# Matmuls of a zeroed tile ahead of and between the first score chunks of an attention and gated feed-forward kernel

## The chip, the cores and the metric

The kernel runs on one core of a Trainium2 chip. The metric is the device time of one launch in microseconds (us). The engines are named as in the profile: PE (TensorE, matmul), PEld (TensorE's loading of weights, which overlaps PE), DVE (VectorE), ACT (ScalarE), POOL (GpSimd) and SP (SyncE, which here issues most of the early DMAs).

## The reference

```python
def _attn_ref(q, k, v) -> np.ndarray:          # (4, 8, 1152, 64) each
    B, H, S, D = q.shape
    factor = 2
    scale = 1.0 / np.sqrt(D)
    q_pool = q.reshape(B, H, S // factor, factor, D).mean(axis=3)
    scores = scale * np.matmul(q_pool, k.transpose(0, 1, 3, 2))
    scores = scores - np.max(scores, axis=-1, keepdims=True)
    attn = np.exp(scores)
    attn = attn / (np.sum(attn, axis=-1, keepdims=True) + 1e-09)
    return np.matmul(attn, v).astype(np.float32)

def _moe_ref(x, w_in, w_out) -> np.ndarray:    # x (2304, 512), d_ff 2048
    h = x @ w_in
    sp = np.where(h > 20.0, h, np.log1p(np.exp(np.minimum(h, 20.0))))
    g = h * np.tanh(sp)
    return (g @ w_out).astype(np.float32)
```

The pooled query gives 576 rows of scores per head against 1152 keys; the attention output of all heads, laid side by side, goes through a feed-forward block.

## The kernel before

The attention is cut into 32 steps: a batch, a pair of heads, and one half of the pooled rows (288 columns a head). Step `i` has nine score chunks of 128 keys each. A chunk (`QK(i, c)`, line 164) is two float32 matmuls, one per head, on the upper and lower half of the array's rows; the trace shows them as four records, two for each head. They write one PSUM tile `s`. ACT copies each chunk to SBUF (`CP`, line 174, into `TA` for chunks 0 to 5 and `TB` for 6 to 8). DVE keeps a running maximum (`MX`, line 185; the last fold `MXF`, line 189). After the ninth chunk PE transposes that maximum (`MT`, line 200, tile `mt`), DVE reduces it (`TMAX`, line 206, tile `m`), PE spreads the result over the partitions (`MB`, line 217, tile `Mb`), DVE subtracts it (`SUB`, line 223), ACT takes the exponential (`EXP`, line 227), and PE multiplies by the values (`PV`, line 246, tile `pv`). Steps overlap: the first chunks of step 1 stand among the last of step 0. A chunk is named (step, chunk) below.

The score tiles have two PSUM buffers (tag `S`); in step 0 chunks 1, 4 and 7 use the buffer that `mt` and `Mb` use later. So a chunk waits until ACT has copied, and DVE has read, the chunk that held its buffer before. The tags `x` and `pv` of the pool `ps1` have one buffer each.

The order on each engine is not found by a scheduler: `mode.enter_context(tc.manual_schedule())` takes the instructions as the program issues them. The program sorts a table of (time, function, arguments), whose first part is `FILL`, and calls the functions in that order. `first()` runs ahead of it:

```python
x = ps1.tile([P, 4, P], F32R, tag="x", name="warm")
for n in range(NWARM):
    pe.transpose(x[:, n % 4], identr, identr)
```

`identr` is an identity that POOL makes and DVE casts. Between the copies of the first chunks ACT, DVE and POOL also convert the first pieces of the feed-forward weights (`conv`, lines 347 to 396, tile `ri` and `wt`), which come by DMA. The steps of the attention take the first half of the time, the feed-forward (float32r matmuls, lines 433 to 727) the rest, with some overlap.

Of the kernel before, what the change touches and what calls it, by code (L numbers as in the profile page):

```python
# [8 lines left out]
F32 = mybir.dt.float32  # L9
F32R = mybir.dt.float32r  # L10
# [13 lines left out]
def tile_pooled_attention_then_winograd_ffn(ctx: ExitStack, tc: tile.TileContext, q, k, v, moe_w_in, moe_w_out, out, outT):  # L24
# [5 lines left out]
    P = 128  # L30
# [8 lines left out]
    NU = NT // UT  # L39
    GR = ((0, 2), (2, 4), (4, 6), (6, 9))  # L40
    CA = GR[3][0]
    NWARM = 19
    TW = 768
    TH = TW // 2
    KT = TW // P
# [4 lines left out]
    pe, dve, act, pool, sp = nc.tensor, nc.vector, nc.scalar, nc.gpsimd, nc.sync  # L50

    const = ctx.enter_context(tc.tile_pool(name="const", bufs=1))
    identr = const.tile([P, P], F32R, name="identr")
    cst = const.tile([P, 2], F32, name="cst")
    one, eps = (cst[:, n:n + 1] for n in range(2))
    xT = const.tile([P, NP, NT], F32, name="xT")

# [5 lines left out]
    def open_pool(name, bufs, side="left", space=bass.MemoryType.SB):  # L63
        shut[name] = ExitStack()
        pools[name] = shut[name].enter_context(
            tc.tile_pool(name=name, bufs=bufs, side=side, space=space, reuse_waits="tile")
        )
        return pools[name]

    mode = ExitStack()  # L70
    mode.enter_context(tc.manual_schedule())
    if True:
        act.preload_act_table_set("natural_log_exp_and_others")
        make_identity(nc, xT[:, 0, 0:P])
        dve.tensor_copy(identr, xT[:, 0, 0:P])
# [25 lines left out]
        ps1 = open_pool("ps1", 1, side="right", space=PSUM)  # L101
# [29 lines left out]
        def qk_tiles(p):  # L131
            qT = pqk.tile([P, 2, HQ], F32, tag="qT", name=f"qT{p}")
            kT = pqk.tile([P, NC, P], F32, tag="kT", name=f"kT{p}")
            qk[p] = (kT, qT)
# [5 lines left out]
        def QH(n):  # L140
            (pool if n in QHP else dve).tensor_tensor(qk[0][1][:, n], raw[0][:, n, 0], raw[0][:, n, 1], ALU.add)

        def first():
            qk_tiles(0)
            if NWARM:
                x = ps1.tile([P, 4, P], F32R, tag="x", name="warm")
                for n in range(NWARM):
                    pe.transpose(x[:, n % 4], identr, identr)

        rmaxs, Mbs, pvs, pvn, accs = {}, {}, {}, {}, {}  # L150
        CHAIN, SEED, FOLD = ((1, 3, 5, 7), (4, 6, 8)), (0, 2), 8
# [6 lines left out]
        def QK(i, c):  # L158
            p, hf = divmod(i, 2)
            kT, qT = qk[p]  # L160
            spare = i == 0 and c in SPARE
            s = (ps1 if spare else psS).tile([P, 2, 512], F32, tag="Mb" if spare else "S", name=f"s{i}_{c}")
            for j in range(2):
                pe.matmul(  # L164
                    s[:, j, 0:HQ],
                    kT[64 * j:64 * j + 64, c],
                    qT[64 * j:64 * j + 64, hf],
                    start=True,
                    stop=True,
                )  # L170
            ss[i, c] = s[:, :, 0:HQ]

        def CP(i, c):
            act.copy(T(i, c), ss[i, c])  # L174
# [568 lines left out]
        for n, u in enumerate(units):  # L743
            if u[0] == 0:
                banks[u] = ("b", "a", "c") if n % 2 else ("a", "b", "c")
            else:
                x, y, z = banks[units[n - 1]]
# [35 lines left out]
        def reuse_lead():  # L783
# [9 lines left out]
            (-0.3930, QH, 0),  # L793
            (-0.3740, load_w, 0),
            (-0.3510, QK, 0, 0),
            (-0.2560, QK, 0, 1),
            (-0.2360, CP, 0, 0),
            (-0.2160, load_q, 0, 1),
            (-0.1770, QK, 0, 2),
            (-0.1570, CP, 0, 1),  # L800
            (-0.1270, load_w, 1),
# [1765 lines left out]
        for u in units:  # L2567
            if 2 <= u[1] <= NFP - 2:
                for t, fn, *a in STEADY[u[0] > 0]:
                    a = (4 * u[1] + a[0], a[1]) if fn is conv else (u, *a)  # L2570
                    if (fn, *a) not in alone:
                        plan.append((NS + (at + t) / PER, fn, *a))
            at += SPANS[u[0] > 0]
        first()
        plan.sort(key=lambda e: e[0])
        for _, fn, *a in plan:
# [40 lines left out]
```

## Time and profile before

| | us |
|---|---|
| median of 3 runs | 785.08 |
| lowest and highest of them | 784.74, 788.81 |
| the profiled execution's own time | 784.51 |
| its span, first to last instruction | 782.7 |
| PE busy in the span | 767.4 (98%) |
| DVE, ACT, POOL busy | 680.6, 642.1, 654.3 |

The span is 1.8 us shorter than the profiled execution's time. A share of busy time is an average over the whole; the change touches only the first 20 us or so, where PE is less busy than later: the first of the 40 slices of the page (19.6 us each) shows seven tenths for PE, all later ones nine but the last. The profile also gives the clock that TensorE was granted, as a share of 2.4 GHz: 1.00 is 2.4 GHz and 0.50 is 1.2 GHz. The ends of matmuls are modelled, so a matmul's duration is longer than the step from one to the next.

### The profile page before, as it was taken

The numbers are of one execution on the slowest core, as the hardware profiler recorded it, in microseconds if no ns is written. First come the engines' busy times: TensorE is split into PE (matmuls) and PEld (weight loads), VectorE is DVE, ScalarE is ACT, GpSimd is POOL, SyncE is SP. The second block draws the span as 40 slices with busy tenths as digits, with TensorE's granted clock in tenths as the row PEclk, the third lists the DMA queues.
The fourth block names the chain that finished last, engine by engine and source line by source line (L and its number), as shares of the span: only waits on it lengthen the run. The fifth ranks groups of instructions, "written<-read, shape, count | busy, mean of one in ns | idle before, by whom it ended". The sixth has DMA issues, their size and how long they took to land.

```text
span 782.7 us, 14324 instructions
## 1 busy us (share of the span) xinstructions
PE 767.4 (98%) x5123; PEld 558.1 (71%) x5123; DVE 680.6 (87%) x959; ACT 642.1 (82%) x1110; POOL 654.3 (84%) x505
## 2 busy tenths in 40 slices
PE   7999999999999999999999999999999999999998
PEld 5454555545555454555557988899899999999998
DVE  5999999999999999999976778877778889587876
ACT  6999999999999999999885887777677687877762
POOL 4679988989889898988887598886788899998884
PEclk9899999999999999999999999999999999999999
DMA  7556575565755656455432788874664232254242
GB/s 269 166 152 142 176 176 116 143 151 138 181 111 149 152 137 170 116 148 116 111 69 46 241 277 290 284 257 172 192 210 151 95 121 69 95 172 142 95 132 101
DMA packets 44470, 121.90 MB, mean 156 GB/s; under 512 B 4592, under 2 KB 16368, under 8 KB 44400
## 3 DMA queue, kind: packets, MB, share of 16 engines
q1 hardware_dynamic: 34608, 71.45, 27.5%
q0 software_dynamic: 4608, 28.31, 18.4%
q10 hardware_dynamic: 5184, 21.24, 8.0%
q8 instruction: 40, 0.66, 0.3%
q14 instruction: 30, 0.25, 0.1%
HBM read 70.65 MB, written 22.02 MB: 118 GB/s over the span
## 4 chain that ended last, share of the span: by engine, by line
PE 86%; DVE 3%; ACT 3%; DMA 3%; POOL 2%; issue 1%; SPq 0%; ACTq 0%; DVEq 0%; POOLq 0%
PE s L164 20%; PE pv L246 17%; PE ma L616 11%; PE O L727 8%; PE OAy L678 7%; PE mc L616 6%; PE O L678 6%; PE mb L616 3%; PE Sb L268 2%; DMA acc<-TB 2%; PE mt L200 2%; PE h L433 1%; PE Mb L217 1%; PE OZ L710 1%; POOL acc L238 1%
## 5 line engine op out<-in xcount | busy, mean ns | idle before, releaser
L164 PE MATMUL s<-qT,kT 64*128 64x288 f32 x1152 | 205.4, 454 | 4.0 <-ACT TB L174 1.8
L164 PEld LDWEIGHTS s<-qT,kT 64*128 64x128 f32 x1152 | 94.0, 189 | 99.8 <-DVE rmax L185 24.9
L174 ACT COPY TA<-s 128x576 f32<-128x576 f32 x192 | 117.9, 638 | 22.9 <-PE s L164 16.5
L223 DVE TENSOR_TENSOR TA<-TA,Mb 128x1152 f32<-128x1152 f32 x96 | 128.9, 1347 | 1.9 <-PE Mb L217 1.0
L227 ACT ACTIVATE TA<-TA 128x1152 f32<-128x1152 f32 x96 | 112.8, 1176 | 4.1 <-DVE TA L223 3.6
L246 PE MATMUL pv<-TA,vn 128*64 128x288 f32 x768 | 115.2, 422 | 0.8 <-ACT TA L227 0.8
L232 POOL TENSOR_TENSOR acc<-TA 128x1152 f32<-128x1152 f32 x32 | 85.0, 2656 | 36.2 <-PE s L164 19.1
L185 DVE TENSOR_TENSOR rmax<-s,rmax 128x576 f32<-128x576 f32 x128 | 93.3, 749 | 2.1 <-ACT TB L174 1.8
L238 POOL TENSOR_TENSOR acc<-acc 128x576 f32<-128x576 f32 x64 | 91.9, 1436 | 3.9 <-DMA acc<-TB 2.6
L246 PEld LDWEIGHTS pv<-TA,vn 128*64 128x64 f32 x768 | 47.2, 137 | 48.5 <-issue 9.7
L691 DVE TENSOR_TENSOR xT<-xT,OAy 128x384 f32<-128x384 f32 x104 | 54.7, 548 | 11.9 <-PE OAy L678 11.6
L223 DVE TENSOR_TENSOR TB<-TB,Mb 128x1728 f32<-128x1728 f32 x32 | 62.2, 1944 | 0.0
L246 PE MATMUL pv<-TB,vn 128*64 128x288 f32 x384 | 61.3, 415 | 0.0
L174 ACT COPY TB<-s 128x576 f32<-128x576 f32 x96 | 59.8, 654 | 1.8 <-PE s L164 1.7
L598 POOL TENSOR_TENSOR wbl<-wS,wbh 128x1024 fp32r<-128x1024 f32 x20 | 49.5, 2476 | 5.8 <-ACT wbh L594 5.8
L227 ACT ACTIVATE TB<-TB 128x1728 f32<-128x1728 f32 x32 | 52.7, 1648 | 0.0
L185 DVE TENSOR_TENSOR rmax<-s,TA 128x576 f32<-128x576 f32 x64 | 48.3, 755 | 3.8 <-ACT TA L174 3.7
L234 POOL TENSOR_TENSOR acc<-TA 128x576 f32<-128x576 f32 x32 | 45.6, 1424 | 2.5 <-ACT TA L227 2.3
L246 PEld LDWEIGHTS pv<-TB,vn 128*64 128x64 f32 x384 | 24.0, 136 | 25.2 <-issue 11.9
L598 POOL TENSOR_TENSOR wal<-wS,wah 128x768 fp32r<-128x768 f32 x19 | 36.8, 1936 | 3.3 <-ACT wah L594 3.1
L598 POOL TENSOR_TENSOR woal<-wO,woah 128x1024 fp32r<-128x1024 f32 x13 | 31.4, 2415 | 7.9 <-ACT woah L594 6.4
L620 ACT COPY s<-ma 128x384 f32<-128x384 f32 x44 | 21.2, 482 | 20.2 <-PE ma L616 20.2
(305 smaller groups left out, 2241.3 us busy)
## 6 DMA issues: line engine op xcount, KB each, us to landing
acc<-TB POOLq DMA_DIRECT2D x32, 864.0 KB, 6.4
ri<-in_moe_w_in_dram SPq DMA_DIRECT2D x16, 512.0 KB, 4.6
ro<-in_moe_w_out_dram SPq DMA_DIRECT2D x16, 512.0 KB, 4.2
qn<-in_q_dram ACTq DMA_DIRECT2D x12, 576.0 KB, 5.0
kT<-in_k_dram ACTq DMA_DIRECT2D x12, 576.0 KB, 3.8
vn<-in_v_dram ACTq DMA_DIRECT2D x12, 576.0 KB, 4.1
wS<-sumsh SPq DMA_DIRECT2D x12, 512.0 KB, 4.0
wO<-sumso SPq DMA_DIRECT2D x13, 384.0 KB, 4.4
```

The costliest lines, as they stand in the source:

```text
L164: pe.matmul(s[:, j, 0:HQ], kT[64 * j:64 * j + 64, c], qT[64 * j:64 * j + 64, hf], start=True, stop=True,)
L174: act.copy(T(i, c), ss[i, c])
L185: dve.tensor_tensor(ss[i, c] if c == FOLD else r, ss[i, c], x, ALU.max)
L223: dve.tensor_tensor(x, x, Mbs[i].unsqueeze(1).to_broadcast([P, w, W]), ALU.subtract)
L227: act.activation(x, x, AF.Exp, scale=0.0625)
L232: pool.tensor_tensor(accs[i][:, 0:2], T(i, 0, 2), T(i, 2, 4), ALU.add)
L238: pool.tensor_tensor(accs[i][:, 0], accs[i][:, 0], accs[i][:, n - 2], ALU.add)
L246: pe.matmul(pvs[i][64 * j:64 * j + 64, 0:HQ], vn[:, j, c, :], T(i, c)[:, j], start=(pvn[i] == 1), stop=(pvn[i] == NC),)
L598: (dve if e == "dve" else pool).tensor_tensor(l, w_part(u, q), f32(h), ALU.subtract)
L616: pe.matmul(o, a, b, start=(new and m == 0), stop=(last and m == len(seq) - 1), skip_group_check=True)
L678: pe.matmul(o, x, y, start=(n == 0 and i not in CHAIN_O[1:]), stop=(n == 2 and i not in CHAIN_O[:3]), skip_group_check=True)
L727: pe.matmul(o, x, y[:, f], start=(f == 0 and m == 0), stop=(f == 1 and m == 2))
```

## The change

A tile `zeros` of 128 by 128 float32r is set to zero by DVE as its first instruction. The 19 transposes of the identity ahead of the first chunk become 29 matmuls of `zeros` by `zeros`. They write a tile on the tag `pv` in place of `x`. The same matmuls are then issued in groups behind seven of the first chunks: 4 behind (0,4), 6 behind (0,5), 6 behind (0,6), 8 behind (0,7), 8 behind (1,0), 10 behind (0,8) and 12 behind (1,1), 54 in all. Nothing reads what they write.

```diff
-    NWARM = 19
+    NWARM = 29
+    FILLER = {(0, 4): 4, (0, 5): 6, (0, 6): 6, (0, 7): 8, (1, 0): 8, (0, 8): 10, (1, 1): 12}
...
+    zeros = const.tile([P, P], F32R, name="zeros")
...
+        dve.memset(zeros.bitcast(F32), 0.0)
         act.preload_act_table_set("natural_log_exp_and_others")
...
+        turns = []
+
         def first():
             qk_tiles(0)
-            if NWARM:
-                x = ps1.tile([P, 4, P], F32R, tag="x", name="warm")
-                for n in range(NWARM):
-                    pe.transpose(x[:, n % 4], identr, identr)
+            warm(NWARM)
+
+        def warm(k):
+            if not turns:
+                turns.append(ps1.tile([P, 4, P], F32, tag="pv", name="warm"))
+            for n in range(k):
+                pe.matmul(turns[0][:, n % 4], zeros, zeros, start=True, stop=True)
...
             ss[i, c] = s[:, :, 0:HQ]
+            warm(FILLER.get((i, c), 0))
```

PE's order at the start of the program, before. `s0_4` is the score tile of chunk (0,4); `warm` is the tile that the first matmuls write.

```order
L164 MATMUL s0_0_196<-qT0_166,kT0_167 128x288 x2
L164 MATMUL s0_1_199<-qT0_166,kT0_167 128x288 x2
L164 MATMUL s0_2_204<-qT0_166,kT0_167 128x288 x2
L164 MATMUL s0_3_212<-qT0_166,kT0_167 128x288 x2
L164 MATMUL s0_4_218<-qT0_166,kT0_167 128x288 x2
L164 MATMUL s0_5_226<-qT0_166,kT0_167 128x288 x2
```

The same place on PE after the change, with the row ahead of it.

```order
L156 MATMUL warm_170<-zeros_60 128x128 x29
L172 MATMUL s0_0_208<-qT0_168,kT0_169 128x288 x2
L172 MATMUL s0_1_211<-qT0_168,kT0_169 128x288 x2
L172 MATMUL s0_2_216<-qT0_168,kT0_169 128x288 x2
L172 MATMUL s0_3_224<-qT0_168,kT0_169 128x288 x2
L172 MATMUL s0_4_230<-qT0_168,kT0_169 128x288 x2
L156 MATMUL warm_170<-zeros_60 128x128 x4
L172 MATMUL s0_5_242<-qT0_168,kT0_169 128x288 x2
```

The first five chunks stand as they did, behind 29 matmuls in place of 19 transposes; the first group follows the fifth chunk.

PE's order from chunk (0,6) to the transposes of step 0's maximum (`mt0`), before.

```order
L164 MATMUL s0_6_235<-qT0_166,kT0_167 128x288 x2
L164 MATMUL s0_7_244<-qT0_166,kT0_167 128x288 x2
L164 MATMUL s1_0_251<-qT0_166,kT0_167 128x288 x2
L164 MATMUL s0_8_255<-qT0_166,kT0_167 128x288 x2
L164 MATMUL s1_1_263<-qT0_166,kT0_167 128x288 x2
L200 MATMUL mt0_277<-identr_58,rmax0_0_210 128x64 x10
```

The same place on PE after the change.

```order
L172 MATMUL s0_6_257<-qT0_168,kT0_169 128x288 x2
L156 MATMUL warm_170<-zeros_60 128x128 x6
L172 MATMUL s0_7_272<-qT0_168,kT0_169 128x288 x2
L156 MATMUL warm_170<-zeros_60 128x128 x8
L172 MATMUL s1_0_287<-qT0_168,kT0_169 128x288 x2
L156 MATMUL warm_170<-zeros_60 128x128 x8
L172 MATMUL s0_8_299<-qT0_168,kT0_169 128x288 x2
L156 MATMUL warm_170<-zeros_60 128x128 x10
L172 MATMUL s1_1_317<-qT0_168,kT0_169 128x288 x2
L156 MATMUL warm_170<-zeros_60 128x128 x12
L209 MATMUL mt0_343<-identr_58,rmax0_0_222 128x64 x10
```

No chunk has changed its place among the others; each of these five now has a group behind it, and nothing but the score chunks' own waits stands between. ACT, POOL and SP issue the same instructions in the same order as before; DVE has one more, the memset, as its first.

## Rows read from the trace of the kernel before

**Rows 1.** The page: span, busy time, slices, and the chain of waits.

```profile
span 782.7 us, 14324 instructions
...
PE   7999999999999999999999999999999999999998
...
PEclk9899999999999999999999999999999999999999
...
PE 86%; DVE 3%; ACT 3%; DMA 3%; POOL 2%; issue 1%; SPq 0%; ACTq 0%; DVEq 0%; POOLq 0%
```

**Rows 2.** Chain of waits in order of time: start us, us, what.

```profile
2.59 5.47 DMA ri<-in_moe_w_in_dram
...
50.31 2.09 PE pv L246 x16
...
57.05 1.61 PE pv L246 x12
```

**Rows 3.** Timeline of PE: start us, us, work, idle before and its releaser.

```profile
1.62 2.65 PE L148 MATMUL warm<-identr 128*128 128x128 f32 x19 [1.62 <-DVE cst L78]
...
4.20 2.29 PE L164 MATMUL s<-qT,kT 64*128 64x288 f32 x8
...
9.40 0.76 PE L164 MATMUL s<-qT,kT 64*128 64x288 f32 x4 [0.62 <-ACT TA L174]
...
15.57 0.76 PE L200 MATMUL mt<-identr,rmax 64*128 64x64 f32 x10 [1.38 <-DVE rmax L189]
16.17 1.19 PE L164 MATMUL s<-qT,kT 64*128 64x288 f32 x8
...
21.36 1.23 PE L246 MATMUL pv<-TA,vn 128*64 128x288 f32 x4 [0.83 <-ACT TA L227]
22.52 2.15 PE L164 MATMUL s<-qT,kT 64*128 64x288 f32 x8
```

**Rows 4.** Windows: stretch, its length, PE busy (instructions), granted clock, DMA share, GB/s.

```profile
7.40:10.70 3.30, 2.58 (x18) 1.00 0.88 357
10.80:14.10 3.30, 2.72 (x16) 1.00 0.59 187
14.20:17.50 3.30, 1.78 (x18) 1.00 0.97 342
17.60:21.00 3.40, 2.83 (x17) 0.50 0.94 305
21.00:24.30 3.30, 2.94 (x12) 0.50 0.19 75
24.50:28.00 3.50, 3.50 (x26) 1.00 0.06 8
393.00:396.40 3.40, 1.55 (x14) 1.00 0.17 33
```

**Rows 5.** Timeline of ACT from 8 us.

```profile
8.09 0.78 ACT L347 ACTIVATE wt<-ri 128x512 uint16<-128x512 uint16 x1 [0.91 <-DMA ri<-in_moe_w_in_dram]
...
13.26 0.67 ACT L174 COPY TB<-s 128x576 f32<-128x576 f32 x1
14.24 0.64 ACT L174 COPY TA<-s 128x576 f32<-128x576 f32 x1 [0.31 <-PE s L164]
...
19.61 0.64 ACT L174 COPY TA<-s 128x576 f32<-128x576 f32 x1 [0.62 <-PE s L164]
```

**Rows 6.** Timeline of DVE.

```profile
13.96 0.77 DVE L185 TENSOR_TENSOR s<-s,rmax 128x576 f32<-128x576 f32 x1 [0.33 <-ACT TB L174]
...
18.54 2.62 DVE L223 TENSOR_TENSOR TA<-TA,Mb 128x1152 f32<-128x1152 f32 x2 [0.23 <-PE Mb L217]
...
24.57 1.58 DVE L185 TENSOR_TENSOR rmax<-s,rmax 128x576 f32<-128x576 f32 x2 [0.68 <-ACT TB L174]
```

**Rows 7.** Chain of waits in the feed-forward: float32r matmuls of 256 and 512 columns.

```profile
427.56 5.75 PE h L433 x48
...
499.94 2.80 PE O L727 x12
```

## The prediction

> **What bounds the kernel now.** I read the page first. PE carries 86% of the chain of waits and is nine tenths busy in every slice but the first and the last [rows 1]. From some 50 us on PE is never short of work: four more records on the chain always cost it 0.48 us (2.09 for 16 less 1.61 for 12) [rows 2]. So time won or lost in the first 30 us shifts all that follows, and nothing else in the change reaches beyond it. The reader should look for what PE, ACT and DVE wait for in those 30 us, and at PE's clock there.
>
> The granted clock is the second thing. It is 1.00 from 7.4 to 17.5 us, 0.50 (1.2 GHz) from 17.6 to 24.3, then 1.00 again [rows 4]. The profile also gives 1.00 for the first 7 us, but there durations say otherwise: eight score records from 4.20 took 2.29 us, as long as the 2.15 us at 22.52 under 0.50, while eight records at 16.17 took 1.19 [rows 3]. So the first chunks ran at 1.2 GHz too. Before the clock fell at 17.5, PE was busy 1.78 of 3.3 us with 18 instructions, ten of them small transposes, after a wait of 1.38 us for DVE; before the other fall, at 396.4, it was busy 1.55 of 3.4 us. In the two stretches from 7.4 and 10.8, with 2.58 and 2.72 us, the clock stayed [rows 3, 4].
>
> The third thing is what holds the first 16 us. The chain goes through the DMA of the first weight piece, which lands at 8.06 us [rows 2]. ACT stands on it until 8.09 with the copies of chunks (0,2) and (0,3) queued behind [rows 5]. After that ACT copies chunk after chunk; the copy of (0,8) starts at 13.26, DVE folds that chunk at 13.96, then the last maximum, and PE's transposes start at 15.57 [rows 3, 5, 6].
>
> **The change part by part.** My sums are made against the profiled execution (784.51 us: the span of 782.7 and 1.8 around it), which is 0.6 us under the median of 785.08.
>
> *29 matmuls for 19 transposes.* The transposes start at 1.62, behind POOL's identity and DVE's casts and memsets, and 19 of them take 2.65 us, at most 0.14 each [rows 3]. The new ones need only DVE's first memset, so I let them start at about 1.0. At half clock 128 columns take 0.107 us, and I bound a matmul by that and the transposes' 0.14: 29 of them end between 4.1 and 5.1 us, and the first chunk started at 4.20. That is a delay of 0 to 0.9 us for the first chunks, or a gain if the clock rises earlier. Either is hidden: ACT must wait for the weight piece until 8.09, and (0,2) and (0,3) are done by then. I take 0. The memset itself stands in front of a cast that waits for POOL's identity anyway, and the new PSUM tag has no other user before the first `pv` matmul at 21.36: 0.
>
> *What one matmul in a group costs.* No float32r matmul of 128 columns stands in the trace. At full clock 48 of 256 columns take 5.75 us, 0.120 each; 12 of 512 take 2.80, 0.233 each [rows 7]. Continued to 128 columns that is 0.120 - 0.057 = 0.063 us. The lower bound is 128 columns at 2.4 GHz, 0.053; the upper is the float32 rate: a score or `pv` matmul of 288 columns takes 0.48 us [rows 2], so 128 columns take 0.213. I take 0.064, since the float32r rows are the same kind of operand. The Trainium skill (TensorE: Matmul & The Clock Gate, Back-to-back issue gap) gives about 81 ns for N=128 in a stream of weight loads and matmuls; no run here shows it yet. By it the next sum would be 0.5 us larger.
>
> *The groups' delay.* A chunk from rest takes 0.76 us to its modelled end [rows 3] and each further one 0.48. Chunk (0,5) cannot start before 9.40, when ACT's copy frees its buffer. From there PE has (0,5), (0,6), (0,7), (1,0) and (0,8), now with 6, 6, 8 and 8 fillers between: 9.40 + 0.76 + 4 x 0.48 + 28 x 0.064 = 13.87. The copy of (0,8) would start at about 13.9 in place of 13.26 [rows 5]: 0.65 late. With 10 more fillers (1,1) ends near 15.0, and its copy, which stood at 14.24 [rows 5], is 0.8 late; ACT's two weight conversions queue behind it, then DVE's conversion, then the reduction of the maximum. The 12 last fillers end near 15.6, before the delayed maximum (16.2), so they cost nothing. The group behind (0,4) lies in PE's wait before 9.40. The delay is 0.8 us; at 0.053 a filler it is 0.5, at 0.213 see the last rival.
>
> *The clock.* If PE stayed at 2.4 GHz from 17.6 to 24.3: `Mb` and the chunk behind it come about 0.3 us sooner, taking DVE's wait of 0.23 before the subtraction and ACT's 0.62 at 19.61 with them [rows 5, 6]. The first `pv` (1.23) and the two chunks at 22.52 (2.15) halve: 1.5 us less on PE [rows 3]. DVE holds part of that back: it is busy from 18.54 on but for 0.68 us before 24.57 [rows 6], so the chain gains about 0.3 + 0.7 + 0.1 = 1.1 us, at most the 1.8 that PE alone would save.
>
> Does it stay? In the stretch that ended at 17.5, the transposes had little beside them; now the 22 last fillers and (1,1) lie there, so I expect 1.00 to hold on past 17.6. But the groups end with (1,1). The next stretch holds `Mb`, two chunks and a wait for the exponential: 2.83 us of work at half clock [rows 4], half of that at full clock, and so less than the 1.78 us that went before the fall at 17.5. I expect the clock to fall there, near 21 us, and the `pv` matmul and the two chunks at 22.52, the dear ones, to run at 1.2 GHz again. Then only some 0.3 of the 1.1 us is won, and work from 24.5 to 28 that ran at 1.00 before may run at half clock for a while, up to 0.8 us lost.
>
> Sum: +0.8 for the groups, -0.3 for the clock, 0 to +0.8 behind: +0.5 to +1.3 on 784.51, so 785.0 to 785.8. I say 785.3.
>
> **The rivals.** *The clock stays up until PE is full.* For it: 3.50 of 3.50 us busy from 24.5 on [rows 4], and the delay of 0.8 us by the groups moves real work into later stretches. Against it: the thin stretch above. Time: 784.51 + 0.8 - 1.1 = 784.2, and 783.9 at the lower price of a filler.
>
> *The zeros do not hold the clock*, because what they stream counts for nothing; no row shows matmuls of zeros. Then it falls at 17.5 again, or sooner: if the first chunks come earlier, (0,4) leaves the stretch from 7.4 and thins it. Time: 784.51 + 0.8 = 785.3 if it falls where it did, and about 787 with the chunks around 11 to 14 us at half clock as well (four of them at 0.48 more each).
>
> *Slower: a float32r matmul of so few columns runs at the float32 rate*, 0.213 us. It would be the groups that decide, between 9.40 and the transposes at 15.57. (0,8) would end at 9.40 + 0.76 + 1.92 + 5.96 = 18.0, and (1,1) with 22 more fillers at 18.0 - 0.2 + 0.48 + 4.7 = 23.0: the transposes 7.4 us late. The 29 ahead would take 6.2 to 12.4 us from 1.0 and add up to 3 us, and 1.1 would come back from the clock: 791 to 795, say 793. Slower than before by over 0.5% it is from about 0.15 us a filler. Against it stands that the transposes, also 128 columns of float32r, took at most 0.14 each at half clock [rows 3], where one pass is 0.107 and four are 0.43.
>
> **How the numbers follow.** Forecast 0.52, the clock staying up 0.24, zeros that do not hold it 0.11, the float32 rate 0.09; 0.04 for something that I have not seen. Half a per cent, about what a measurement of this kernel can tell from no change, is 3.9 us: 781.2 to 789.0. The first three cases lie inside, so "same" holds 0.87; slower is the float32 rate and the end of the third case, 0.10; faster 0.03. The range goes from 783.3, the clock staying up with PE's own saving in place of DVE's (784.51 + 0.8 - 1.8, less a little), to 788.2, the third case with a filler of 0.08. The likeliest case's own range is 784.5 to 786.3.
>
> **What would show it.** In the changed profile a group of eight fillers should take 0.5 us at full clock; the copy of (0,8) should start near 13.9 and the transposes near 16.3; PEclk should be 1.00 over 17.6 to 20.9 and 0.50 in a stretch after it. If the copy of (0,8) stays at 13.3 the groups are free and I have their price wrong; if no 0.50 stands before 30 us the first rival is right; if a group of eight takes 1.7 us the last one is. The first five chunks should be earlier or later without the 8.09 of ACT moving.

## The result and the profile after

The changed kernel took 792.44 us (median of 6 runs, 790.73 to 797.38) against 784.91 for the kernel before (median of 6, 782.70 to 788.81): a ratio of 1.0121, 95% interval 1.0095 to 1.0147. It is slower by about 1%: two of the six runs lay at 797 and lift the ratio, the two medians alone give 1.0096. The prediction had said 785.3 and "same". Run again beside the experiments (e11 below) it took 791.09, a ratio of 1.0095, 1.0081 to 1.0109. The profiled execution took 791.35 us; its span of 789.4 is 6.7 us longer than the 782.7 of before.

The page of the kernel after, the rows that answer to [rows 1] (slices, and the chain by engine and by line):

```profile
span 789.4 us, 14453 instructions
...
PE   9899999999999999999989999999999999999998
...
PEclk9999999999999999999999999999999999999999
...
PE 87%; POOL 4%; ACT 3%; DVE 3%; DMA 2%; issue 1%; ACTq 0%; DVEq 0%; POOLq 0%
PE s L172 20%; PE pv L255 16%; PE ma L625 11%; PE O L736 7%; PE OAy L687 7%; PE mc L625 6%; PE O L687 6%; PE mb L625 3%; PE Sb L277 2%; POOL acc L247 2%; PE warm L156 2%; PE mt L209 2%; PE h L442 1%; DMA acc<-TB 1%; PE OZ L719 1%
```

The first slice is full now (9 where a 7 stood), and matmuls of zeros hold 2% of the chain. PE's timeline shows where they stand (start us, us, work; in brackets idle time before it and what ended it; no row before 25 us but the first gives any). It answers to [rows 3].

```profile
1.06 6.45 PE L156 MATMUL warm<-zeros 128*128 128x128 f32 x29 [1.06 <-DVE zeros L75]
7.43 4.58 PE L172 MATMUL s<-qT,kT 64*128 64x288 f32 x20
11.94 0.66 PE L156 MATMUL warm<-zeros 128*128 128x128 f32 x4
12.54 0.76 PE L172 MATMUL s<-qT,kT 64*128 64x288 f32 x4
13.22 0.89 PE L156 MATMUL warm<-zeros 128*128 128x128 f32 x6
...
17.95 1.11 PE L156 MATMUL warm<-zeros 128*128 128x128 f32 x8
18.99 0.76 PE L172 MATMUL s<-qT,kT 64*128 64x288 f32 x4
19.67 1.33 PE L156 MATMUL warm<-zeros 128*128 128x128 f32 x10
20.93 0.76 PE L172 MATMUL s<-qT,kT 64*128 64x288 f32 x4
21.62 1.56 PE L156 MATMUL warm<-zeros 128*128 128x128 f32 x12
23.11 0.76 PE L209 MATMUL mt<-identr,rmax 64*128 64x64 f32 x10
...
35.66 0.76 PE L209 MATMUL mt<-identr,rmax 64*128 64x64 f32 x10 [0.62 <-DVE rmax L198]
```

The first chunk starts at 7.43 in place of 4.20, chunk (0,5) at 12.54 in place of 9.40, and the transposes of step 0's maximum at 23.11 in place of 15.57. Those of step 1 come at 35.66; before they stood at 29.72:

```profile
29.72 0.76 PE L200 MATMUL mt<-identr,rmax 64*128 64x64 f32 x10 [0.74 <-DVE rmax L189]
```

The chain of waits runs through the zeros (start us, us, what):

```profile
12.61 0.69 PE s L172 x4
13.29 0.82 PE warm L156 x6
...
16.29 1.04 PE warm L156 x8
17.33 0.69 PE s L172 x4
...
19.74 1.26 PE warm L156 x10
```

Two more matmuls of zeros cost 0.22 us each time, so one costs 0.11; a group of n holds 0.15 + 0.11 n of the chain, and each chunk 0.69 where chunks that follow one another take 0.48. ACT has become the engine that waits, which answers to [rows 5]: the weight piece, chunk (0,8), chunk (1,1).

```profile
10.31 0.79 ACT L356 ACTIVATE wt<-ri 128x512 uint16<-128x512 uint16 x1
...
19.79 0.64 ACT L183 COPY TB<-s 128x576 f32<-128x576 f32 x1 [1.08 <-PE s L172]
21.73 0.64 ACT L183 COPY TA<-s 128x576 f32<-128x576 f32 x1 [1.31 <-PE s L172]
```

The windows, answering to [rows 4]: stretch, length, PE, PEld, DVE, ACT and POOL busy, granted clock, DMA share, GB/s.

```profile
13.70:17.10 3.40, 3.40 (x26) 2.49 (x25) 1.84 (x4) 2.08 (x4) 1.41 (x1) 1.00 1.01 401
17.10:20.50 3.40, 3.40 (x26) 2.49 (x25) 0.71 (x2) 1.28 (x2) 0.00 (x0) 1.00 0.28 104
...
24.00:27.40 3.40, 2.69 (x25) 1.27 (x21) 3.40 (x5) 2.56 (x5) 1.63 (x2) 1.00 0.80 283
27.40:31.00 3.60, 2.60 (x18) 1.18 (x20) 3.60 (x5) 3.58 (x5) 2.75 (x2) 1.00 0.10 42
...
403.00:406.40 3.40, 3.40 (x14) 1.88 (x16) 2.92 (x3) 3.02 (x6) 3.32 (x3) 0.50 0.00 0
```

PE is busy without a gap until the transposes at 23.1, and the clock stays at 1.00 where before it stood at 0.50; it falls only at 403 us. In exchange DVE and ACT, which carry the real work, have little to do: 0.71 and 1.28 us of the 3.4 from 17.1.

### The profile page after: what moved, and what is told of

It is laid out like the page before. It is cut to its first block, busy times and chain, and to the rows that moved or that the text cites. A ratio compares the mean times of both kernels' runs of the same rounds, so it can differ in the third digit from the quotient of the medians.

```text
span 789.4 us, 14453 instructions
## 1 busy us (share of the span) xinstructions
PE 776.1 (98%) x5187; PEld 566.8 (72%) x5187; DVE 682.1 (86%) x960; ACT 642.7 (81%) x1110; POOL 654.2 (83%) x505
## 4 chain that ended last, share of the span: by engine, by line
PE 87%; POOL 4%; ACT 3%; DVE 3%; DMA 2%; issue 1%; ACTq 0%; DVEq 0%; POOLq 0%
PE s L172 20%; PE pv L255 16%; PE ma L625 11%; PE O L736 7%; PE OAy L687 7%; PE mc L625 6%; PE O L687 6%; PE mb L625 3%; PE Sb L277 2%; POOL acc L247 2%; PE warm L156 2%; PE mt L209 2%; PE h L442 1%; DMA acc<-TB 1%; PE OZ L719 1%
```

## The experiments

My first theory was that a matmul of zeros costs what loading its 128 weight columns costs, that the groups are the larger part of the slowdown, and that most of the lead (the 29 matmuls ahead) is hidden. The rivals: that the streamed columns set the price, and that the late start is carried on whole. The table gives for each kernel how much later than before the transposes of the maximum start in step 0, 1, 12 and 28, and the span's end, in its profiled execution; and in the columns POOL and PE how long, between 100 and 395 us, POOL waited for its accumulating DMA (`acc<-TB`) and PE's `Sb` matmuls then waited for POOL.

| kernel | step 0 | step 1 | step 12 | step 28 | end | POOL | PE |
|---|---|---|---|---|---|---|---|
| before | 0 | 0 | 0 | 0 | 0 | 2.2 | 0.6 |
| after | 7.54 | 5.95 | 6.14 | 6.21 | 6.70 | 3.6 | 1.6 |
| e1, lead alone | 3.02 | 2.52 | 2.51 | 4.19 | 2.80 | 6.7 | 2.6 |
| e2, groups alone | 5.34 | 3.76 | 5.00 | 4.46 | 5.41 | 0.6 | - |
| e3, 64 weight columns | 2.52 | 1.47 | 1.74 | 1.92 | 1.61 | 3.6 | 1.6 |
| e4, 64 streamed columns | 7.65 | 6.10 | 6.42 | 6.50 | 6.68 | 3.5 | 1.6 |
| e5, all transposes | 3.56 | 4.58 | 4.58 | 4.04 | 3.80 | 0.6 | - |
| e6, bfloat16 | 2.35 | 2.26 | 7.28 | 7.41 | 7.45 | 3.7 | 1.7 |
| e7, two groups in waits | 0.11 | -1.42 | -0.92 | 0.76 | 1.40 | 8.2 | 3.2 |
| e8, one group | 0.45 | -1.09 | -1.08 | 0.04 | 0.15 | 5.1 | 1.5 |
| e9, 15 ahead | 1.93 | 1.31 | 1.30 | 0.74 | 0.70 | 0.6 | - |
| e10, nothing ahead | 0.58 | 0.21 | 0.21 | -0.31 | -1.25 | 0.6 | - |
| e11, after again | 7.54 | 5.95 | 6.01 | 6.25 | 5.93 | 3.7 | 1.8 |
| e12, e6 and a buffer | 2.33 | 2.32 | 2.34 | 2.46 | 3.39 | 3.5 | 1.6 |

The column of the end carries more than the change. In six of these profiles (before, after, e2, e4, e6, e7) the clock fell once more, for 3.4 us, between 396 and 409 us. The other eight, where it did not, all gained 1.4 us on the kernel before between the transposes of steps 30 and 31. The changed kernel is on both sides (after and e11), so the code does not fix this. The column of step 28 stands ahead of it.

**e1: the lead alone.**

```diff
-    FILLER = {(0, 4): 4, (0, 5): 6, (0, 6): 6, (0, 7): 8, (1, 0): 8, (0, 8): 10, (1, 1): 12}
+    FILLER = {}
```

> Only the 29 zero matmuls ahead, no groups. In the changed kernel they took 6.45 us from 1.06 and the first chunk started at 7.43 in place of 4.20. Theory (the groups are the larger part of the loss, and most of the lead's delay is hidden by ACT's wait for the weight piece until 8.09): chunk (0,5) starts at 10.6 to 11.6 in place of 9.40, the transposes of the maximum at 16.7 to 17.8 in place of 15.57, and the time is 784.5 to 786. Rival (the late start is carried on whole): the transposes 3 us late, 787 to 788.

787.41 us against 784.09, ratio 1.0043 (1.0024 to 1.0061), and the transposes 3.02 late: my theory fell, the rival held. The 29 end as in the changed kernel and the first chunk starts at 7.43. ACT in e1:

```profile
8.81 0.64 ACT L183 COPY TA<-s 128x576 f32<-128x576 f32 x1 [6.79 <-PE s L172]
9.77 0.64 ACT L183 COPY TA<-s 128x576 f32<-128x576 f32 x1 [0.32 <-PE s L172]
10.31 0.79 ACT L356 ACTIVATE wt<-ri 128x512 uint16<-128x512 uint16 x1
```

The conversion of the weight piece, which I had used as the cover, came 2.22 us late (10.31 for 8.09) without waiting for its DMA any more, because two copies of late chunks stand ahead of it in ACT's queue. The cover was never the time until 8.09, only the 0.91 us that ACT was idle there [rows 5]: 3.2 us of lateness less 0.9 is about what is left of it there. But the conversion does not set the 3.02 us. The chain of waits in e1 passes it by: it runs from the zeros through the first four chunks to a fold of DVE, and from there to ACT's copies.

```profile
7.50 4.07 PE s L172 x16
...
11.60 0.77 DVE rmax L194
...
12.39 0.64 ACT TA L183
```

The late chunks are slow as well, for in this run the clock rose only at 11.3 us (in the changed kernel at 10.5, before at 7.3).

**e2: the groups alone.** The 19 transposes stand ahead again, the 54 zeros stay.

```diff
-            warm(NWARM)
+            x = ps1.tile([P, 4, P], F32R, tag="x", name="lead")
+            for n in range(19):
+                pe.transpose(x[:, n % 4], identr, identr)
```

> The 19 identity transposes ahead as before, and the 54 zero matmuls in groups. Theory: a group of n costs PE 0.34 + 0.112 n us at full clock, so (0,8) starts near 15.9 in place of 12.35 and the transposes of the maximum near 20.0 to 20.9 in place of 15.57; some 1.3 us come back if the clock stays at 1.00 to 30 us, which leaves 787.5 to 789. Rival (the late start is the larger part): the groups cost under 2 us, 784.5 to 786.5.

787.78, ratio 1.0041 (1.0023 to 1.0059), and the transposes at 20.91, as the theory said. The clock stayed at 1.00 from 6.0 us to 402. The two halves add up within their intervals: 1.0043 x 1.0041 is 1.0084, some 6.6 us, against 1.0095 (1.0081 to 1.0109) for the whole in e11. The first theory's order was wrong: lead and groups cost the same. One thing in e2's profile is not the groups' price: its shift grows by 1.2 us between steps 1 and 2 (3.76 to 4.99), where POOL stands 1.9 us. Run e6 shows what that is.

**e3 and e4: which half of the pair sets the price.** e3 loads 64 weight columns and streams 128; e4 loads 128 and streams 64.

```diff
-                pe.matmul(turns[0][:, n % 4], zeros, zeros, start=True, stop=True)
+                pe.matmul(turns[0][0:64, n % 4], zeros[:, 0:64], zeros, start=True, stop=True)    # e3
+                pe.matmul(turns[0][:, n % 4, 0:64], zeros, zeros[:, 0:64], start=True, stop=True) # e4
```

> As the changed kernel, but each zero matmul loads 64 weight columns in place of 128; it still streams 128. Theory (loading the weights sets the step, 256 clocks for 128 float32r columns): the step halves, to about 0.107 us at half clock and 0.056 to 0.067 at full clock; the 29 end near 4.2 and the time is 785 to 787. Rival (a float32r matmul of 128 streamed columns takes two passes or the time of 256 columns): the step stays 0.213 and 0.112, and the time 790 to 793.

> As the changed kernel, but each zero matmul streams 64 columns in place of 128; it still loads 128 weight columns. Theory (loading the weights sets the step): the step stays 0.213 us at half clock and 0.112 at full clock, and the time 790 to 793. Rival (two passes over the streamed columns): the step falls to about 0.107 and 0.056, and the time to 785 to 787. If it stays here and in the run with 64 weight columns as well, a least time for any such matmul is left.

e3 took 786.96, ratio 1.0062 (1.0030 to 1.0094); two of its eight runs lay at 794, the other six at 785.8 to 788.8, much as two of six did in the changed kernel; neither kernel has a profile of such a run. e4 took 791.65, ratio 1.0087 (1.0062 to 1.0112), in three runs. PE's timeline, the lead and the groups of 4 and 12; first e3, then e4:

```profile
1.06 3.35 PE L156 MATMUL warm<-zeros 128*64 128x128 f32 x29 [1.06 <-DVE zeros L75]
...
8.47 0.46 PE L156 MATMUL warm<-zeros 128*64 128x128 f32 x4
...
17.12 0.93 PE L156 MATMUL warm<-zeros 128*64 128x128 f32 x12
```

```profile
1.06 6.39 PE L156 MATMUL warm<-zeros 128*128 128x64 f32 x29 [1.06 <-DVE zeros L75]
...
12.27 0.63 PE L156 MATMUL warm<-zeros 128*128 128x64 f32 x4
...
21.77 1.52 PE L156 MATMUL warm<-zeros 128*128 128x64 f32 x12
```

Eight more matmuls in a group cost 0.90 us in the changed kernel (1.56 less 0.66), 0.47 with half the weight columns, 0.89 with half the streamed ones. So for this pair the load sets the price, at both levels of the clock: the lead halves with the weight columns and does not move with the streamed ones.

**e5 and e6: the same groups of another kind.** In e5 all of them, ahead and between, are transposes of the identity (19 ahead); in e6 `zeros` is bfloat16.

```diff
-                pe.matmul(turns[0][:, n % 4], zeros, zeros, start=True, stop=True)
+                pe.transpose(turns[0][:, n % 4], identr, identr)                  # e5
-    zeros = const.tile([P, P], F32R, name="zeros")
+    zeros = const.tile([P, P], mybir.dt.bfloat16, name="zeros")               # e6
```

> The same places and counts as the changed kernel, but every zero matmul is a transpose of the identity (19 ahead as before, 54 in the groups). If what costs is loading the weights of a plain float32r matmul, the transposes, which stepped by 0.127 us at half clock where the zero matmuls step by 0.213, step by 0.06 to 0.08 at full clock, the transposes of the maximum start at 17.9 to 18.9 in place of 20.9 with zero matmuls, and the time is 785 to 787. Rival (any instruction pair in a group costs 0.11, whatever it loads): 20.9, and 787 to 789.

> The changed kernel with a bfloat16 zero tile in place of float32r: 29 ahead and 54 in groups. If the load of the weights takes its time by the float32r kind (256 clocks for 128 columns), bfloat16 halves it or better: the step is 0.107 to 0.13 at half clock and 0.055 to 0.07 at full clock, the first chunk starts at 4.2 to 4.6, and the time is 785 to 787.5, as with 64 weight columns. Rival (128 weight columns take 256 clocks in any type): 0.213 and 0.112, 790 to 793.

e5: 787.43, ratio 1.0049 (1.0034 to 1.0064). It lies between its two cases: a transpose steps by 0.085 us, above the 0.06 to 0.08 of the theory and under the 0.11 of the rival, and the transposes of the maximum start at 19.13. A transpose loads as many weight columns of the same type as a matmul of zeros does, so the number of columns is not the whole price. e6: 790.22, ratio 1.0085 (1.0055 to 1.0114), far above the 785 to 787.5 that I expected, though its price per matmul is as expected: 29 take 3.27 us, and twelve less four take 0.44, or 0.055 each. The table shows where it went: 5.0 us between steps 1 and 12, of which 4.6 fall between steps 1 and 2. e6's chain of waits there, and the time that spills took to land, before and in e6:

```profile
33.62 2.70 DMA spill<-wt
36.32 4.67 issue
40.99 2.12 POOL wt L358
43.12 2.56 POOL acc L241
...
45.70 0.65 ACT TA L183
```

```profile
DMA to landing us min/median/max: 2.0/2.2/2.4
...
DMA to landing us min/median/max: 2.9/5.1/7.2
```

POOL's next conversion writes a buffer that a spill to memory still reads; the spill took up to 7.2 us to land where before it took 2.4, POOL stood 4.7 us, its sums behind it came late, and ACT's copies waited for those. (The view names no releaser for POOL's wait; 33.6 and 7.2 us make 40.8, just ahead of 40.99.) In e2 the slower spill took 4.4 us and POOL stood 1.9. That was read from the times alone, so I tested it.

**e12: e6, with a buffer of its own for that conversion.**

```diff
-                wt[n] = wraw_p.tile([P, DM], F32, tag="wt", name=f"wt{n}") if n < 4 else w32((0, n // 4), n % 4)
+                wt[n] = (wraw_p.tile([P, DM], F32, tag="wt2", name=f"wt{n}", bufs=1) if n == 2 else wraw_p.tile([P, DM], F32, tag="wt", name=f"wt{n}")) if n < 4 else w32((0, n // 4), n % 4)
```

> The bfloat16 zeros again, and POOL's third converted weight piece has a buffer of its own, so that it no longer waits until the spill of an earlier piece has landed. Theory (the 5 us between the second and the third maximum were POOL standing 4.7 us for the spill, and the copies, the chunks and the maximum behind it): no such wait, the shift against before stays near 2.3 us after step 2, and the time is 785 to 787.5 with no run above 790. Rival (the late spill is only a sign of crowded transfers, and something else comes late in its place): the shift after step 2 is 5 us or more again and runs above 790 remain.

787.91, ratio 1.0044 (1.0024 to 1.0064), 785.45 to 789.63 in nine runs. The shift stays at 2.3 us. The spill landed as late as in e6, and POOL did not wait; the row for the tile `spill`, and POOL's timeline:

```profile
DMA to landing us min/median/max: 3.0/5.1/7.3
```

```profile
36.36 2.14 POOL L358 TENSOR_SCALAR wt<-ro 128x512 uint16<-128x512 uint16 x1
```

So the wait for the late spill is shown as the cause of the 5 us in e6's profile. In the medians the buffer is worth 2.3 us, with intervals that just overlap: e6's four runs go from 786.87 to 792.12, so that not every execution lost the 5 us. The time lies 0.4 us above what I expected.

**e7 and e8: groups only where PE waits anyway.** Both keep the 19 transposes.

```diff
-    FILLER = {(0, 4): 4, (0, 5): 6, (0, 6): 6, (0, 7): 8, (1, 0): 8, (0, 8): 10, (1, 1): 12}
+    FILLER = {(1, 1): 9, (1, 5): 6}   # e7
+    FILLER = {(1, 1): 9}              # e8
```

> The 19 identity transposes ahead as before, and groups of zero matmuls only where PE waited 1.4 us before the transposes of the maximum (9 behind (1,1), 0.34 + 9 x 0.112 = 1.35 us) and before the first pv matmul (6 behind (1,5), 1.0 us). Theory (groups hold the clock; they cost only where they stand in no wait): the transposes of the maximum of step 0 stay at 15.5 to 15.7, the clock stays 1.00 to 30 us, those of step 1 start at 28.1 to 28.5 in place of 29.72, and the time is 1.1 to 1.6 us under before's, a ratio of 0.998 to 0.999. Rival (the groups do not hold the clock, or it falls anyway in the next stretch): those of step 1 at 29 to 29.8, and no difference.

> As the run with groups in the two waits, but only the 9 behind (1,1). If the clock falls one stretch later than before, near 21 us, as the prediction had it: the transposes of the maximum of step 1 start near 29.0 and the clock is 0.50 for 3.4 us from about 21. If the one group is enough: 28.1 to 28.5, and no 0.50 before 30 us.

785.92, ratio 1.0027 (1.0010 to 1.0044), and 785.19, ratio 1.0015 (0.9997 to 1.0032): neither beats the kernel before, and e7, which I expected 0.1 to 0.2% faster, is a little slower. In both the clock stayed at 1.00 past 17.6 us, and step 1's maximum came 1.42 and 1.09 us earlier; the table shows that this was given back between steps 8 and 28. The waits from 100 to 395 us (total us, times, longest), first of the kernel before, then of e7:

```profile
POOL acc L238 <- DMA acc<-TB: 2.2, 3, 1.6
...
PE Sb L268 <- POOL acc L238: 0.6, 1, 0.6
```

```profile
POOL acc L249 <- DMA acc<-TB: 8.2, 6, 1.6
...
PE Sb L279 <- POOL acc L249: 3.2, 5, 0.7
```

Six times, not three, an accumulating DMA landed after POOL was ready, and five times PE stood for POOL; the 2.6 us more on PE cover the 2.2 us by which the shift grew from step 1 to 28. In the table the larger losses between steps 12 and 28 go with such waits (e1, e7, e8), and where PE has none the shift falls by 0.5 us, about the 0.6 that the kernel before loses (e2, e5, e9, e10). What makes the DMA late at one shift and not at another was not tried.

**e9 and e10: how much lead does no harm.** Fifteen zeros ahead, and none; no groups.

```diff
-    NWARM = 29
+    NWARM = 15   # e9; 0 in e10
-    FILLER = {(0, 4): 4, (0, 5): 6, (0, 6): 6, (0, 7): 8, (1, 0): 8, (0, 8): 10, (1, 1): 12}
+    FILLER = {}
```

> Fifteen zero matmuls ahead in place of 29, no groups. By 0.213 us each at 1.2 GHz, which the 29 took, fifteen run from 1.06 to about 4.3, as long as the 19 transposes did. Theory (the lead costs only by where it ends): first score chunk at 4.2 to 4.4, the transposes of step 0's maximum within 0.3 us of 15.57, and the time within 0.1% of before, 784 to 785.5. Rival (zeros ahead are worse for the clock than transposes, whatever their end): the clock rises later than before, the transposes of the maximum come 1 us late or more, and the time is 786 or more.

> Nothing ahead of the first chunk and no groups. DVE's qT, which the first chunk needs, ended at 4.08 in the trace before. Theory (the lead neither raises the clock nor delays anything as long as it ends by 4.2): first chunk at 4.1 to 4.2 and the time within 0.15% of before. Rival (19 transposes ahead bring the rise of the clock forward): without them the first chunks at half clock last longer, the transposes of the maximum come 0.5 to 2 us late, and the time is 785.3 to 786.5.

782.96, ratio 0.9993 (0.9971 to 1.0015), and 783.33, ratio 0.9989 (0.9968 to 1.0010): both the same as before. In e9 the first chunk starts at 4.45. Its profiled execution, with 785.34 the slowest of its ten, has the transposes 1.93 us late, not within the 0.3 that I expected: in it the weight piece came only at 9.28, which is where its chain of waits runs through, and the clock fell at 10.8 and again at 17.6. That is one of the rival's signs without its cause (the clock rose at 7.4) and without its time. e10's timeline of PE:

```profile
4.04 4.58 PE L172 MATMUL s<-qT,kT 64*128 64x288 f32 x20 [4.04 <-DVE qT L144]
...
16.15 0.76 PE L209 MATMUL mt<-identr,rmax 64*128 64x64 f32 x10 [1.38 <-DVE rmax L198]
```

The first chunk waits for `qT` until 4.04. A lead that lets the first chunk start by 4.45 costs nothing, and buys nothing, that these runs can tell.

**e11: the changed kernel again.**

> The changed kernel again, for its spread: four of its six runs lay at 790.7 to 792.5 and two at 797.2 and 797.4. Theory (the lead and the groups are all of it, and the two high runs are a late transfer that an execution meets or not): most runs at 790 to 793, median 791 to 792.5, some runs about 5 us higher. Rival (something steady is missing from the sum of the parts): a median of 793.5 or more with few runs under 791.5.

790.60 to 791.53 in four runs, span 788.7. The two runs of 797 in the first six did not come again; no profile shows one, so whether they met something like e6's wait is open. These runs show nothing steady that is missing from the sum.

## Why the prediction was wrong

**What bounds the kernel: right.** Time lost in the first 30 us was carried on whole, 5.95 us at step 1 and 6.70 at the end. "Nothing else in the change reaches beyond it" was too strong: later transfers came late or in time as the start had shifted, worth from 0.5 us won (e9) to 4.6 us lost (e6).

**The price of one matmul: the step that failed.** I continued the line through 256 and 512 streamed columns down to 128 and took 0.064 us. It measured 0.11 at 2.4 GHz and, in the lead, 0.22 at 1.2 GHz ((7.43 - 1.06) / 29). The line has a floor that neither row could show: the load of 128 weight columns takes 0.11 us, less than the 0.120 for 256 streamed columns [rows 7], but more than streaming 128 or 64 (e3, e4). My upper bound of 0.213 for a filler held, and I chose the low end because the operands were of the same kind; the shape decided. The Trainium skill gives 81 ns for N=128 (TensorE: Matmul & The Clock Gate, Back-to-back issue gap). Of the two it was nearer, but not enough to change the forecast; the measured float32r pair costs more, 112 ns, the bfloat16 pair less, 55.

**The lead: failed by the same price.** "29 of them end between 4.1 and 5.1" became 7.4, since I took 0.107 to 0.14 each. And "either is hidden" had a cover of only 0.9 us, on ACT alone; the folds of DVE, which wait for the same chunks, had another path past it (e1). At 0.25 us of lateness the time did not move (e9); at 3.2 us it cost 3.0 us at the transposes (e1).

**The groups' delay: 0.8 us forecast, 4.4 measured** (23.11 - 12.54 against 15.57 - 9.40). From the start of (0,5) to the modelled end of (0,8) my sum was 0.76 + 4 x 0.48 + 28 x 0.064 = 4.47; the timeline gives 18.99 + 0.76 - 12.54 = 7.21. Of the 2.74 more, 28 x 0.048 = 1.34 are the price of a matmul. The other 1.4 is 0.35 for each of four groups, a term I did not have: 0.15 at the group's end, and 0.21 because a chunk behind a group takes 0.69 in place of 0.48. That the copy of (1,1), two conversions, DVE's and then the reduction stand in line was right: the chain runs that way. That the group behind (0,4) lies in a wait of PE was not: behind the late lead PE had no wait left there, and the group holds 0.59 us of the chain. Nor did the twelve last fillers end ahead of the maximum: they ended at 23.1, DVE's last fold at 22.0. The chain passes them by through ACT, so here this cost nothing. The lower case of the same sum was off too: at 0.053 a filler 0.4 us follows, not 0.5, since 38 fillers stand ahead of (1,1) and not 28.

**The clock: wrong, to the other side.** I expected a fall near 21 us and 0.3 us of gain. After the rise at 10.5 us no 0.50 stands before 403, and from the transposes of step 0 to those of step 1 it takes 12.55 us in place of 14.15: 1.6 us won, where I had put 1.1 and at most 1.8. In e7 and e8, where the clock stayed up too and the transposes of step 0 came at most 0.45 us late, the same stretch won 1.5. The thin stretch that I had counted on did not come: from 24.0 to 27.4, with `Mb` and the chunks around it, PE was busy for 2.69 us with 25 instructions, where I had counted on half of the 2.83 us of 17 [rows 4]. This was my first rival's mechanism. Together: 3.1 at (0,5), where the lead and the first group have told, 4.4 for the other groups, 1.6 back, 5.9 at step 1.

**The rivals and the chances.** The time fell into the last rival's case, 791 to 795, which I gave 0.09. Its transposes 7.4 us late are the measured 7.54, but that is luck: it put all of them down to groups at 0.213 a filler. At 2.4 GHz a filler cost half of that and the groups 4.4; the other 3.1 had arisen by (0,5), most of it from the late lead. Of the 29 ahead it said that they take 6.2 us or more and add up to 3, and that was so. What I should have asked of the profile is what a pair of load and matmul takes when both are short. The transposes ahead were such pairs, and the nearest row by shape: [rows 3] gave 0.14 at 1.2 GHz, or 0.07 if halved for 2.4. Even that would have been low, by about a third at either level of the clock.

## What to carry to other kernels

A filler matmul is a weight load and a stream, and for the float32r zeros here the longer of the two was the price: take it from rows of the same shape, type and kind, not from wider ones, and add what a group costs the work behind it. Filler that keeps the clock up can pay only in time that PE spends waiting, and here even that came to nothing in the end (e7, e8); put between real chunks it delays the engines that the chain runs through. "Hidden behind a wait" is worth the idle time in front of that wait, with what is queued ahead of it, not the time at which the wait ends, and only if no other engine passes the lateness on.

## What the runs showed of the hardware

- Pairs of 128 by 128 with a load for each matmul: float32r 0.22 us at 1.2 GHz and 0.11 at 2.4; with 64 weight columns 0.11 and 0.06; bfloat16 0.055 and float32r transposes 0.085 at 2.4 GHz. Why a transpose of the same size is cheaper than a matmul was not tried.
- 6.4 us of zeros ahead did not bring the clock's rise forward. By the durations of PE's records it rose at 10.1 to 12.0 us in the four profiles with 29 such matmuls of 128 weight columns ahead (after, e1, e4, e11), and at 5.7 to 7.6 in the other ten, with transposes, fewer or shorter matmuls or nothing (e10, 7.6) ahead. Counted from the start of the first score chunk it rose 1.4 to 4.6 us later in all fourteen, whatever stood ahead. Single executions scatter: 7.3 before and 6.0 in e2, where PE's instructions up to there are the same.
- With groups of float32r zeros the clock, once up, did not fall before 398 us in any of the profiles (after, e2, e3, e4, e7, e8, e11); without groups it fell between 10.8 and 25.0 in all four (before, e1, e9, e10), with transposes or bfloat16 at 23.3 to 24.2 (e5, e6, e12). In e8's profile one group of nine was enough. Each is one profile, two for the changed kernel.
- With shifts of a few microseconds at the start other DMAs landed late: a spill in 2.0 to 7.3 us, accumulating DMAs that held POOL for 0.6 to 8.2 us in all between 100 and 395 us.
- A fall of the clock for 3.4 us near 400 us came and went between two executions of the same kernel (after, e11) and cost 1.4 us.
